# Attention matmuls in 64x64 tiles, and the fourth sequence loaded head by head, in a fused retention and feed-forward kernel

## The chip, the cores and the metric

The kernel runs on one core of a Trainium2 chip. The metric is the device time of one execution in microseconds (us), as the median of several runs. A core has five engines with instruction streams of their own: PE (TensorE, matrix products), DVE (VectorE), ACT (ScalarE), POOL (GpSimd) and SP (SyncE, which here only issues DMAs), and 16 DMA engines that they share.

## The reference

A decayed linear attention (retention) is followed by a feed-forward block with the activation h + sin(alpha h)^2 / alpha.

```python
# q, k, v: (4, 8, 768, 64) float32; gamma[h] = 1 - 2**(-5-h); scale = 1/8
for t in range(S):
    state = gamma * state + k[:, :, t] (outer) v[:, :, t]
    y[:, :, t] = scale * q[:, :, t] @ state
x = y as (4*768, 512)
h = x @ w_in                       # 512 x 2048
s = sin(alpha * h)
out = (h + s * s / (alpha + 1e-9)) @ w_out     # 2048 x 512
```

The recurrence is computed in chunks: within a chunk as masked scores times v, across chunks through a 64x64 state per head.

## The kernel before, in words

**Chunks and groups.** Each of the 4 sequences is cut into 6 chunks of 128 tokens, 24 chunks in all, for all 8 heads at a time. `order` (P in the code) holds the first chunk of each sequence (e0 to e3 = P[0] to P[3]), then the other five of sequence 0 (P[4] to P[8]), of sequence 1 (P[9] to P[13]), 2 and 3 (P[19] to P[23]). The feed-forward block works on seven groups of consecutive chunks of that order, of 4, 2, 4, 4, 4, 4 and 2 chunks. The order of instructions on each engine is written out by hand, with no scheduler.

**Attention of a chunk.** q and k are cast to bf16 on the way in and transposed to [2 heads x 64, 128 tokens], either on PE with an eviction (`half_T`, `stage_T`) or by a DMA transpose that SP issues (`turn`, X in the schedule). `stage_A` (L207, A) makes the scores, 8 matmuls that contract over 64 rows (L213), and DVE masks them out of PSUM into bf16 (L217). `stage_M` (L236, M) multiplies the state, held as a 128x128 block-diagonal matrix of two heads in bf16 (`s_bd`), with q (L247, 8 matmuls of 128 rows and 64 columns), adds the masked scores times v (L251, 8 matmuls), then adds k times v to the running state in a PSUM bank of its own (`stage_S`, L227, 8 matmuls). DVE scales the result by the decay table into xT (L258), and ACT copies the state to `s_bd` (L234, two copies of 64 partitions). v is multiplied beforehand by a decay factor (`scale_v`, L112), mostly on POOL. `SK` does the state sums of a sequence's first chunk.

**Feed-forward.** A `Slot` computes one tile of 128 hidden units for the tokens of a group: 4 matmuls into `ph` (L279), a sine on ACT (L282), a square on ACT or DVE (L287, L289), and one fused multiply-add on DVE into gT (L294, `add`), which frees `ph`. `ff_out` (L304) multiplies gT with w_out into a PSUM bank per chunk; `take` (L309) copies it out on ACT (L316) and SP stores it.

**Order.** `phase` (L375) runs the 16 slots of group g (for a group of 2 chunks, 8 double slots), spreads the output matmuls of group g-1 among them, and in given slots the attention of group g+1: A of a chunk and M of the one before it together, the last M in the last slot but one. Within a slot the order is: matmuls, sine, square, attention, add, output matmuls. Group 0 and what lies up to L515 is written out line by line.

**Loads.** POOL issues nearly all loads: 3 DMAs for a chunk (q, k, v; `load_chunk`), 4 for w_in (`load_w_in`), 4 for w_out. Every one of them reuses one of 8 semaphores and so waits for the landing of the load eight before it. After L486 the loads of P[7] and later chunks stand on POOL between the `scale_v` of earlier chunks.

**PSUM** has 8 banks: 4 rotating ones ("mm": ph, po, transposes), 2 for scores ("pa"), 1 for results and transposes ("ty") and 1 for the running state ("ps").

Of the kernel before, what the change touches and what calls it, by code (L numbers as in the profile page):

```python
# [11 lines left out]
ALU = mybir.AluOpType  # L12
# [3 lines left out]
def kernel(  # L16
# [9 lines left out]
):  # L26

# [45 lines left out]
    def load_chunk(j, names="qkv"):  # L73
        for name, src in (("q", q), ("k", k), ("v", v)):
            if name not in names:
                continue
            if name == "v":
                t = big.tile([128, H, D], BF16, name="vr", tag="vr", bufs=NJ)
            else:
                if ("qk", j) not in raw:  # L80
                    raw["qk", j] = big.tile([128, 2, H, D], BF16, name="qkr", tag="qkr", bufs=NJ)
                t = raw["qk", j][:, "qk".index(name)]
            nc.gpsimd.dma_start(out=t, in_=chunk_of(src, j))  # L83
            raw[name, j] = t

# [4 lines left out]
    def load_w_in(i):  # L90
        nc.gpsimd.dma_start(out=w_in[:, :, i * fw:(i + 1) * fw], in_=w_in_v[:, :, i * fw:(i + 1) * fw])
# [6 lines left out]
    for name, src in (("q", q), ("k", k)):  # L98
        near[name] = big.tile([128, H, D], F32, name=f"{name}0")
# [11 lines left out]
    def scale_v(j, eng):  # L111
        eng.tensor_mul(raw["v", j], raw["v", j], kg[:, j % NCH, :, None].to_broadcast([128, H, D]))  # L112
# [38 lines left out]
    for p in range(NP):  # L151
        for e in range(2):
            nc.vector.memset(lgp[64 * e:64 * e + 64, p:p + 1], lng[2 * p + e])
# [3 lines left out]
                         lg[:, None, :].to_broadcast([128, NCH, H]))  # L157
    qg = consts.tile([128, NCH, NP, C], F32, name="qg")
# [12 lines left out]
    s_bd = [big.tile([128, NP, 128], BF16, name=f"s_bd{i}") for i in range(2)]  # L171
# [3 lines left out]
    xT = {}  # L175

    def half_T(j, i, eng):
# [4 lines left out]
        for p in range(NP):  # L182
            nc.tensor.transpose(pt[:, p, :], raw["qk"[i], j][:, 2 * p:2 * p + 2, :].rearrange("p h d -> p (h d)"), ident)
# [6 lines left out]
    def stage_T(j, eng=None, tag="ty"):  # L190
        pt = psum.tile([128, 2 * NP, 128], BF16, name="pt", tag=tag, bufs=4 if tag == "mm" else 1)
        st["qkT", j] = work.tile([128, 2 * NP, 128], BF16, name="qkT", tag="qkT", bufs=6)
        for i in range(2):
            for p in range(NP):
                nc.tensor.transpose(pt[:, i * NP + p, :],  # L195
                                    raw["qk"[i], j][:, 2 * p:2 * p + 2, :].rearrange("p h d -> p (h d)"), ident)
# [5 lines left out]
    def turn(j):  # L202

        st["qkT", j] = work.tile([128, 2 * NP, 128], BF16, name="qkT", tag="qkT", bufs=6)
        nc.sync.dma_start_transpose(out=st["qkT", j], in_=raw["qk", j].rearrange("p i h d -> p (i h d)"))

    def stage_A(j):  # L207
        qkT = st["qkT", j]
        pa = psum.tile([128, 2, NP, 128], F32, name="pa", tag="pa")
        for p in range(NP):  # L210
            for e in range(2):
                r = slice(64 * e, 64 * e + 64)
                nc.tensor.matmul(pa[:, e, p, :], qkT[r, NP + p, :], qkT[r, p, :],  # L213
                                 start=(p == 0), stop=True, skip_group_check=True)
        aT = work.tile([128, 2, NP, 128], BF16, name="aT", tag="aT", bufs=2)
# [349 lines left out]
```

## Time and profile before

| What | Value |
|---|---|
| median of 8 runs | 219.27 us (218.33 to 219.78) |
| the profiled execution's own time | 218.33 us |
| its span, first to last instruction | 216.6 us |
| granted PE clock | 1.00 throughout |
| DMA | 24.67 MB; the core's DMA engines at 9 tenths or more in the first 21 of 40 slices |
| first feed-forward matmul | 15.3 us |
| first slot of group 1, group 2, group 3, group 4, group 5, group 6 | 47.2, 64.1, 90.0, 122.5, 154.7, 184.6 us |
| last PE matmul ends, about | 212.4 us |

In the profile, L12 is line 12 of the kernel before. Busy times are sums over the instructions of an engine; matmuls are pipelined, so that the time from one start to the next tells more than a duration. A line such as `101.03 0.29 PE L227 MATMUL ps<-vr,qkr 128*64 128x64 bf16 x8` is eight matmuls, the first of which starts at 101.03 us and the last of which ends 0.29 us later; 128*64 are the rows and columns of the array that they use, 128x64 the moving operand.

### The profile page before, as it was taken

The page shows a single profiled execution, that of the slowest core. Times are in us where ns is not written, and L with a number is a line of the kernel's source. Part 1 is how long each engine was busy: PE and PEld are TensorE (multiplying, and loading weights), DVE is VectorE, ACT ScalarE, POOL GpSimd, SP SyncE. Part 2 cuts the span into 40 slices and gives each one's busy share as a digit, 9 for nine tenths or more (in the row PEclk, how much of TensorE's full clock was granted, in tenths as well). Part 3 has the DMA queues.
Part 4 walks back from the last instruction along what each step waited for, and adds up shares of the span by engine and source line. Part 5 has one row for each costly group of instructions (what it writes and reads, how often), then busy time and mean ns, then how long its engine had stood idle before and what let it go on. Part 6 is the DMA issues. An engine that isn't in the chain of part 4 may idle for free.

```text
span 216.6 us, 4245 instructions
## 1 busy us (share of the span) xinstructions
PE 207.6 (96%) x1661; PEld 107.6 (50%) x1661; DVE 128.7 (59%) x213; ACT 162.6 (75%) x311; POOL 90.1 (42%) x105
## 2 busy tenths in 40 slices
PE   7899898999989999999999999999999999999992
PEld 3445543467754545445454545454544544556540
DVE  4688579859896777666367467367464655233300
ACT  7679786758988899788777867877868876766610
POOL 8975335899899895897871000000000000000000
PEclk9999999999999999999999999999999999999999
DMA  9999999999999999999997046125001101111121
GB/s 128 158 197 192 206 207 163 154 206 174 164 149 175 172 137 155 114 162 162 149 185 106 3 94 100 50 49 101 20 30 51 48 0 51 48 48 48 51 96 50
DMA packets 99508, 24.67 MB, mean 114 GB/s; under 512 B 92304, under 2 KB 96416, under 8 KB 99488
## 3 DMA queue, kind: packets, MB, share of 16 engines
q0 software_dynamic: 77024, 13.37, 83.6%
q1 hardware_dynamic: 22464, 11.02, 25.3%
q8 instruction: 13, 0.21, 0.5%
q14 instruction: 7, 0.06, 0.1%
HBM read 27.27 MB, written 6.29 MB: 155 GB/s over the span
## 4 chain that ended last, share of the span: by engine, by line
PE 74%; DMA 12%; POOL 4%; DVE 4%; ACT 2%; issue 1%; POOLq 0%
PE po L304 35%; PE ph L279 31%; DMA qkr<-in_k_dram 8%; DMA w_in<-in_moe_w_in_dram 4%; PE py L247 3%; PE pa L213 2%; POOL qkr L83 2%; PE py L251 2%; DVE aT L217 1%; POOL vr L83 1%; DVE xT L258 1%; PE ps L227 1%; DVE gT L294 1%; PE pt L195 1%; ACT s L282 1%
## 5 line engine op out<-in xcount | busy, mean ns | idle before, releaser
L294 DVE SCALAR_TENSOR_TENSOR gT<-s,rec_alpha,ph 128x512 bf16<-128x512 f32 (+3 forms) x120 | 74.2, 638 | 68.0 <-ACT s L287 67.4
L304 PE MATMUL po<-w_out,gT 128*128 128x512 bf16 x384 | 98.5, 380 | 0.6 <-DVE gT L294 0.6
L279 PE MATMUL ph<-xT,w_in 128*128 128x512 bf16 (+3 forms) x480 | 98.0, 337 | 0.6 <-DVE gT L294 0.2
L282 ACT ACTIVATE s<-ph,alpha_sb 128x512 f32<-128x512 f32 (+3 forms) x120 | 69.6, 601 | 32.9 <-PE ph L279 32.7
L279 PEld LDWEIGHTS <-w_in 128*128 128x128 bf16 x480 | 45.5, 98 | 42.1 <-issue 1.8
L287 ACT ACTIVATE s<-s 128x512 f32<-128x512 f32 (+1 forms) x94 | 58.4, 621 | 2.6
L304 PEld LDWEIGHTS <-gT 128*128 128x128 bf16 x384 | 35.2, 98 | 38.2 <-issue 0.6
L112 POOL TENSOR_TENSOR vr<-vr,kg 128x512 bf16<-128x512 bf16 x21 | 22.0, 1060 | 11.6 <-DMA vr<-in_v_dram 11.6
L217 DVE TENSOR_TENSOR aT<-pa,mask 128x1024 bf16<-128x1024 f32 x20 | 24.4, 1221 | 0.2 <-PE pa L213 0.2
L83 POOL DMA_DIRECT2D vr<-in_v_dram x24 | 21.8, 910 | 4.0 <-DMA w_in<-in_moe_w_in_dram 1.7
L83 POOL DMA_DIRECT2D qkr<-in_q_dram x23 | 21.3, 927 | 3.9 <-DMA w_out<-in_moe_w_out_dram 1.7
L83 POOL DMA_DIRECT2D qkr<-in_k_dram x23 | 20.6, 895 | 3.6 <-DMA w_out<-in_moe_w_out_dram 3.4
L234 ACT CAST s_bd<-ps 64x256 bf16<-64x256 f32 x40 | 14.3, 359 | 2.5 <-PE ps L227 2.2
L316 ACT COPY o_sb<-po 128x512 f32<-128x512 f32 x23 | 13.1, 576 | 4.0 <-PE po L304 3.9
L258 DVE TENSOR_TENSOR xT<-py,qg 128x512 bf16<-128x512 f32 x20 | 13.7, 684 | 2.2 <-PE py L251 2.1
L328 PE MATMUL spare<-warm 128*128 128x512 bf16 x28 | 9.8, 476 | 1.2 <-DVE warm L131 1.2
L213 PEld LDWEIGHTS <-qkT 64*128 64x128 bf16 x192 | 5.4, 94 | 9.3 <-issue 7.1
L251 PE MATMUL py<-aT,vr 128*64 128x128 bf16 x192 | 9.6, 220 | 0.4 <-DVE rec_alpha L366 0.2
L213 PE MATMUL pa<-qkT 64*128 64x128 bf16 x192 | 9.6, 219 | 0.4 <-ACT qkT L186 0.2
L247 PE MATMUL py<-qkT,s_bd 128*64 128x128 bf16 x160 | 8.3, 224 | 0.8 <-DVE xT L258 0.7
L247 PEld LDWEIGHTS <-s_bd 128*64 128x64 bf16 x160 | 5.5, 109 | 4.7 <-issue 2.0
L251 PEld LDWEIGHTS <-vr 128*64 128x64 bf16 x192 | 6.9, 110 | 1.3 <-issue 1.0
(59 smaller groups left out, 69.8 us busy)
## 6 DMA issues: line engine op xcount, KB each, us to landing
out_dram<-o_sb SPq DMA_DIRECT2D x24, 256.0 KB, 2.4
vr<-in_v_dram POOLq DMA_DIRECT2D x24, 128.0 KB, 5.9
qkr<-in_q_dram POOLq DMA_DIRECT2D x23, 128.0 KB, 5.6
qkr<-in_k_dram POOLq DMA_DIRECT2D x23, 128.0 KB, 5.8
w_in<-in_moe_w_in_dram POOLq DMA_DIRECT2D x4, 512.0 KB, 10.1
w_out<-in_moe_w_out_dram POOLq DMA_DIRECT2D x4, 512.0 KB, 14.5
q<-in_q_dram SPq DMA_DIRECT2D x1, 256.0 KB, 3.2
k<-in_k_dram SPq DMA_DIRECT2D x1, 256.0 KB, 4.6
```

The costliest lines, as they stand in the source:

```text
L83: nc.gpsimd.dma_start(out=t, in_=chunk_of(src, j))
L112: eng.tensor_mul(raw["v", j], raw["v", j], kg[:, j % NCH, :, None].to_broadcast([128, H, D]))
L213: nc.tensor.matmul(pa[:, e, p, :], qkT[r, NP + p, :], qkT[r, p, :], start=(p == 0), stop=True, skip_group_check=True)
L217: nc.vector.tensor_mul(aT.rearrange("p e n t -> p (e n) t"), pa.rearrange("p e n t -> p (e n) t"), m)
L247: nc.tensor.matmul(py[r, p, :], s_bd[c % 2][:, p, r], qkT[:, p, :], start=(p == 0), stop=True, skip_group_check=True)
L251: nc.tensor.matmul(py[64 * e:64 * e + 64, p, :], vs[:, 2 * p + e, :], aT[:, e, p, :], start=(c == 0 and p == 0), stop=True, skip_group_che ...
L258: nc.vector.tensor_mul(x, py, qg[:, c])
L279: nc.tensor.matmul(self.ph[:, m, :], w_in[:, i, f * 128:(f + 1) * 128], xT[g][:, i, self.lo:self.hi], start=(m == 0 and i == 0), stop=(i = ...
L282: nc.scalar.activation(out=self.s[:, m, :], in_=self.ph[:, m, :], func=ACTF.Sin, scale=alpha_sb[:, f:f + 1])
L287: nc.scalar.activation(out=self.s, in_=self.s, func=ACTF.Square)
L294: nc.vector.scalar_tensor_tensor(gT[self.g][:, f, self.lo:self.hi], self.s[:, m, :], rec_alpha[:, f:f + 1], self.ph[:, m, :], op0=ALU.mult ...
L304: nc.tensor.matmul(po[g, ts], gT[g][:, f, ts * C:(ts + 1) * C], w_out[:, f, :], start=(f == 0), stop=(f == FF - 1))
```

## The change

Heads get another place. Head 4b + 2m + e is worked on in PSUM bank b, and its 64 output columns lie in half b XOR e, so that the four products of one m (b = 0, 1 and e = 0, 1) use the four quadrants of the array. w_in's rows for heads 4 to 7 are loaded with their 64-partition halves swapped to match: three DMAs in place of one for each of the four parts of w_in. The state is kept in fp32 in SBUF (`s_f`, added to by DVE) and handed on in bf16 as plain 64x64 blocks (`s_n`).

For the five later chunks of the fourth sequence (`wide`), q, k and v are loaded head by head (24 DMAs of 64 partitions), with two sets of 64 tokens on the free axis. Their scores, products and sums are 64x64 tiles, the half of the scores above the diagonal is left out, and the state is a zero-padded 128x128 block (`s_w`), written by POOL.

Scores of a chunk, state product and products of the chunk before and the state sums form one `burst`. The evictions that follow it (`keep`: state sum, `mask`, `exit`: xT, `hand`: the bf16 state) are queued by `phase` in an order of its own for group 1 (`calm=False`): `hand` ahead of the next slot's sine, and the slot's addition ahead of mask and exit. The first state sums (`begin`) move into group 0. P[8] to P[10] are transposed on PE, and stage_T's evictions are on ACT but for e3 and P[6]. scale_v of most chunks goes to DVE, and POOL issues loads with fewer waits. The last output tile is made in three column pieces.

PSUM: 4 "mm", 2 "pa", 2 "py" (results and sums). Some lines without bearing on this are left out; "..." marks the place.

```diff
     def load_w_in(i):
-        nc.gpsimd.dma_start(out=w_in[:, :, i * fw:(i + 1) * fw], in_=w_in_v[:, :, i * fw:(i + 1) * fw])
+        c = slice(i * fw, (i + 1) * fw)
+        nc.gpsimd.dma_start(out=w_in[:, 0:2, c], in_=w_in_v[:, 0:2, c])
+        for y in range(2):
+            nc.gpsimd.dma_start(out=w_in[64 * y:64 * y + 64, 2:4, c], in_=w_in_v[64 - 64 * y:128 - 64 * y, 2:4, c])
+    def load_seq(bt):
...
+        for i, src in enumerate((q, k, v)):
+            for h in range(H):
+                r = slice(64 * (h // NP), 64 * (h // NP) + 64)
+                o = tv[r, :, h % NP, :] if i == 2 else tqk[r, :, i, h % NP, :]
+                nc.gpsimd.dma_start(out=o, in_=src[bt, h, C:, :].rearrange("(f i) d -> i f d", i=64))
...
+    def sums(j, py, base=256):
+        ks, vs = raw["k", j], raw["v", j]
+        for f in range(2 if wide(j) else 1):
+            for m in range(2):
+                for b, e in tiles4:
+                    o = py[half(e), b, base + 64 * m:base + 64 * m + 64]
+                    if not wide(j):
+                        h = 4 * b + 2 * m + e
+                        nc.tensor.matmul(o, ks[:, h, :], vs[:, h, :], ...
+                    else:
+                        nc.tensor.matmul(o, ks[half(b), f, 2 * m + e, :], vs[half(b), f, 2 * m + e, :], ...
+    def keep(j, py, base=256):
+        new = py[:, :, base:base + 128].rearrange("p b (m d) -> p m b d", m=2)
...
+            nc.vector.tensor_add(s_f, s_f, new)
+    def hand_on(j):
+        i = (j % NCH + 1) % 2
+        if not wide(j + 1):
+            nc.scalar.copy(s_n[i], s_f)
+            return
...
+        nc.gpsimd.tensor_copy(s[half(0), :, 0:4:3], s_f[half(0)])
+        nc.gpsimd.tensor_copy(s[half(1), :, 1:3], s_f[half(1)])
+    def inter(j):
...
+        for m in range(2):
+            if wide(j):
+                for b in range(2):
+                    nc.tensor.matmul(py[:, b, m * 128:(m + 1) * 128].rearrange("p (f i) -> p f i", f=2),
+                                     s[:, m, b, :], qkT[:, m:m + 5:4, half(b)], ...
+                continue
+            for b, e in tiles4:
+                nc.tensor.matmul(py[half(b ^ e), b, m * 128:(m + 1) * 128], s[half(e), m, b, :],
+                                 qkT[half(e), 2 * b + m, :], ...
+    def scores(j, tag="pa"):
...
+                for f in range(2):
+                    for e in range(2):
+                        nc.tensor.matmul(pa[half(f), e, p, :], qkT[half(e), NP + p, half(f)], qkT[half(e), p, :], ...
...
+    def burst(old, new, first=None):
+        inter(old)
+        return {**scores(new), **mix(old, first)}
...
+    def last_tile(g, ts):
+        lo = 0
+        for n in (d_model // 2, d_model // 4, d_model // 4):
...
     def phase(...):
         for n in range(FF // nf):
+            more, fresh = rest[0], {}
+            if not calm:
+                run(more, "hand")
             now = Slot(g, n * nf, nf=nf).sq("A")
+            run(more, "keep", "exit", "hand")
             for fn in att.get(n, ()):
-                fn()
-            now.add()
-            while done < no * (n + 1) * nf // FF:
+                fresh.update(fn() or {})
+            if calm:
+                run(fresh, "mask")
+                now.add()
+            else:
+                run(fresh, *(("keep", "exit") if n == FF // nf - 1 else ("keep",)))
+                now.add()
+                run(fresh, "mask", "exit")
...
+            while done < ((no - hold) * (n + 1) * nf // FF if n < FF // nf - 1 else no):
...
+    for j in (e0, e1, e2, e3):
+        scale_v(j, nc.vector)
     a = Slot(0, 0, (n3, n4), 4)
...
     a = Slot(0, 13)
+    begin(e0)
     b.sq("D").add()
...
     load_chunk(P[10])
     scale_v(P[8], nc.gpsimd)
-    scale_v(e1, nc.gpsimd)
...
+    load_chunk(P[11])
+    scale_v(P[9], nc.gpsimd)
+    load_chunk(P[12])
+    load_chunk(P[13])
+    for j in P[14:19]:
+        load_chunk(j)
+    load_seq(3)
...
+    stage_T(P[6])
     fill(3)
-    stage_A(P[5])
-    SK(e0)()
...
+    run(burst(P[4], P[5]), "keep", "hand", "mask", "exit")
+    fill(4)
+    stage_T(P[7], nc.scalar)
     fill(5)
-    stage_M(P[4])
-    fill(4)
-    stage_M(P[5])
+    more = burst(P[5], P[6])
+    run(more, "exit", "keep")
+    stage_T(P[8], nc.scalar)
+    run(more, "hand", "mask")
     fill(4)
     phase(1, outs,
-          {0: [T(P[6]), X(P[8])], 1: [A(P[6])], 2: [T(P[7]), X(P[9])], 3: [A(P[7]), M(P[6])], 4: [X(P[10])],
-           5: [A(P[8]), M(P[7])], 6: [X(P[11]), A(P[9]), M(P[8]), SK(e1)], 7: [M(P[9])]}, 2)
+          {1: [B(P[6], P[7])], 2: [T(P[9])], 3: [B(P[7], P[8])], 4: [T(P[10]), X(P[11])],
+           5: [B(P[8], P[9], e1)], 7: [B(P[9], P[10])]}, 2, calm=False, hold=6)
...
-    for fn in out_pieces(NG - 1, range(sizes[-1])):
+    for fn in out_pieces(NG - 1, range(sizes[-1] - 1)):
         fn()
+    last_tile(NG - 1, sizes[-1] - 1)
```

In the later groups a burst of chunks j and j+1 stands three slots ahead of each quarter's end, the DMA transpose of the chunk two further on two slots before it, and scale_v one slot before it (four in the fourth sequence, on POOL).

## The prediction

> **What bounds the kernel now.** I read the page's first and fourth parts, then TensorE's timeline matmul by matmul, then busy times by stage.
>
> ```profile
> PE 207.6 (96%) x1661; PEld 107.6 (50%) x1661; DVE 128.7 (59%) x213; ACT 162.6 (75%) x311; POOL 90.1 (42%) x105
> PE 74%; DMA 12%; POOL 4%; DVE 4%; ACT 2%; issue 1%; POOLq 0%
> ```
>
> TensorE is busy nearly always and carries 74% of the chain; DMA and POOL carry the head. A busy TensorE may still stream badly, so I take start-to-start times around one attention chunk of group 4 (columns: start, length, engine, line, tiles, shape, count):
>
> ```profile
> 99.28 1.03 PE L279 MATMUL ph<-xT,w_in 128*128 128x512 bf16 x4
> 100.23 0.40 PE L213 MATMUL pa<-qkT 64*128 64x128 bf16 x8
> 100.56 0.41 PE L247 MATMUL py<-qkT,s_bd 128*64 128x128 bf16 x8
> 100.81 0.39 PE L251 MATMUL py<-aT,vr 128*64 128x128 bf16 x8
> 101.03 0.29 PE L227 MATMUL ps<-vr,qkr 128*64 128x64 bf16 x8
> 101.26 1.04 PE L304 MATMUL po<-w_out,gT 128*128 128x512 bf16 x4
> ```
>
> The next feed-forward matmul starts at 102.13. A 512-column matmul costs 0.216 us (four from 101.26 in 0.87). So the chunk costs 102.13 - 99.28 - 8 x 0.216 = 1.12 us. Its parts: L251's eight matmuls take 0.22 us (100.81 to 101.03), while eight unpaired 128-column transposes (L195, in the chain at 48.27) take 0.45: half-array matmuls already run **two at a time**, 0.055 a pair. L227's eight of 64 columns: 0.29 long, 0.196 each, so (0.29 - 0.196) / 7 = 0.0134 us apart. Each change of tile shape costs about 0.1: 0.09 into L213 (100.14 to 100.23), 0.11 out of it (0.33 against 0.22), 0.12 out of L227 (0.23 against 0.11); first weights after one 0.03.
>
> The stages, cut where TensorE starts a slot (columns: stretch, length, busy PE, PEld, DVE, ACT, POOL, clock, DMA):
>
> ```profile
> 37.25:47.23 9.98, 9.84 (x113) 5.21 (x111) 8.31 (x10) 6.29 (x12) 9.04 (x11) 1.00 2.36 174
> 47.23:64.11 16.88, 16.26 (x226) 12.01 (x225) 14.06 (x25) 14.36 (x33) 15.47 (x17) 1.00 2.01 166
> 64.11:89.96 25.85, 25.43 (x216) 12.40 (x216) 18.50 (x25) 22.66 (x41) 21.66 (x24) 1.00 2.03 154
> 89.96:122.45 32.49, 32.49 (x266) 15.80 (x265) 18.67 (x24) 26.07 (x47) 20.54 (x22) 1.00 1.52 135
> 122.45:154.69 32.24, 32.24 (x257) 15.61 (x256) 18.70 (x24) 25.06 (x45) 0.00 (x0) 1.00 0.35 67
> 154.69:184.56 29.87, 29.87 (x186) 13.84 (x185) 15.38 (x20) 23.20 (x39) 0.00 (x0) 1.00 0.10 36
> ```
>
> Subtract the feed-forward matmuls (30, 16 + 64 half-width, 96, 128, 128, 128 of 0.216, half-width at 0.109): 3.5, 6.45, 5.1, 4.9, 4.6 and 2.25 us are left for attention, transposes and waits, 26.8 in all. That, and the tail, is what the change can touch. From 64 us on TensorE alone is the limit; before, loads matter too:
>
> ```profile
> 19.79 17.17 DMA qkr<-in_k_dram
> 37.00 0.40 PE pt L195 x4
> 59.44 0.68 DVE xT L258
> ```
>
> P[4]'s k lands at 36.96 and TensorE, waiting since 35.8, goes on at 37.0. Group 1's slots then lose about 0.9 us to DVE (L258 in the chain).
>
> **The change, part by part.** *Burst of an ordinary chunk.* The state product goes from 8 matmuls in pairs (0.22) to 8 in fours (0.11). The scores stay at 0.22: 16 matmuls in fours instead of 8 in pairs. L251's and L227's successors keep 0.22 and 0.11. Shape changes stay three (0.32), first weights come twice (0.06). Sum 1.04, 0.08 less than 1.12. Four at a time needs one start per 0.014 us, L227's measured pace; that all four quadrants overlap, no row shows. Bounds: 0 extra, or pairs only, 0.33 extra. I take 0, since pairs along rows (L213) and along columns (L251) both overlap here.
>
> The Trainium skill ("TensorEngine Tiling (Array Packing)", Gotcha 1: PSUM Pressure) says that different row tiles cannot access one PSUM bank at the same time. The new state product puts row halves e = 0 and 1 of one b into one bank, on different partitions, which no row here shows. By the rule it would go in pairs and cost 15 x 0.11 = 1.65 us more in all.
>
> *Burst of the fourth sequence.* State product at full array, four matmuls of 0.056 = 0.22, with no shape change ahead; scores and products 0.165 each (8 of 128 and 8 of 64 columns, in fours); sums 0.11; two shape changes 0.21; weights 0.03: 0.90. The 64-column ones would start 0.007 apart, which no row shows; at L227's 0.0134 the 32 of them add 0.22. Bounds 0.90 and 1.12; I take 1.0.
>
> The skill ("TensorE: Matmul & The Clock Gate", Part 1) gives a floor of about 25 ns start to start. L227's 13.4 contradicts it for column tiles, and the measurement decides. By the rule this burst would be some 0.5 us dearer.
>
> *Fewer pieces.* A group now has four closed bursts; before, five (scores alone, three full, L251 alone, 0.44 + 3 x 1.12 + 0.80) and extra sums. By stage:
> - 64.11 to 89.96: 4 x 1.04 = 4.15, and I keep 0.35 of wait (76.89, o_sb): 4.5, gain 0.65.
> - 89.96 to 122.45: 4.15 against 4.9, gain 0.75.
> - 122.45 to 154.69: 4 x 1.0 against 4.6, gain 0.6.
> - 154.69 to 184.56: 1.0 + 0.22 + 0.40 against 2.25, gain 0.6.
>
> *Transposes moved to TensorE.* P[8] to P[10] leave SP's DMA transposes: 3 x 0.45 = 1.35 on TensorE, 3 x 1.01 of copies on ACT. T(P[6]) moves ahead of the first burst and now waits for its load. Transfers follow P[4]'s k about 0.9 us apart (POOL's issues at 36.33, 37.24, 38.15, each released by a landing); P[6]'s k is six later: 37.0 + 5.4 = 42.4. TensorE would be there at 41.25 and wait about 0.95. Work from 37.25: scores alone 0.43, four transposes 1.8, two bursts 2.1, wait 0.95: 5.3 against 3.5, **loss 1.8**. Group 1's slots: 4 x 1.04 + 2 x 0.45, and 0.4 of waits I leave standing, 5.45 against 6.45: gain 1.0. The hold of six output matmuls gives DVE 1.7 us to finish L258's successor ahead of group 2; that removes the wait after 61.3.
>
> *Other engines.* Group 1's slots on ACT: 8 x 1.41 (two sines 0.87, square 0.54), two transpose copies 1.9, four hand-ons at 0.33 (one L234 cast's row), two o_sb 1.0: 15.4. TensorE needs 10.45 + 5.05 = 15.5: level. DVE: 16 x 0.39 + 4 x (1.14 + 0.60 + 0.35) = 14.6, the new 0.35 by the 256-wide rows. In group 2 DVE gains scale_v (0.61 clear of POOL's arithmetic, 1.44 beside it): 16 x 0.67 + 4 x 2.7 + 1.0 for the masks = 22.5 of 25.2. Level or hidden, but with no reserve. In the last groups scale_v and the state copies on POOL have at least four slots (7 us) before their use.
>
> *Head.* Eight more DMA issues on POOL (w_in in thirds, about 0.74 each, 5.9 us) all stand before P[4]'s. Cover: w_in and w_out land at DMA's pace, not POOL's; P[4]'s k was issued at 19.79 and landed 17 us later, so up to about 6 us are hidden. If a 64-partition transfer were half as fast, the eight halves would cost 5 us: no row; I take 0, as the packets are the same. begin(e0) (0.31) and a DVE state copy (0.35) lie in the wait before 37.0; four scale_v (2.4) fit DVE's idle 24.7 to 27.3. I put 0.2 for what leaks. The fourth sequence's 24 issues end near 95 us at 0.75 each; its first transpose comes near 112.
>
> *Tail.*
>
> ```profile
> 203.63 8.80 PE L304 MATMUL po<-w_out,gT 128*128 128x512 bf16 x40
> 212.46 0.42 DVE L313 COPY o_sb<-po 128x256 f32<-128x256 f32 x1 [6.23 <-PE po L304]
> 212.92 0.37 ACT L314 COPY o_sb<-po 128x256 f32<-128x256 f32 x1 [3.33 <-DVE o_sb L313]
> ```
>
> Two serial copies (0.83) become one of 128 columns (0.42 - 0.13 = 0.29); 48 narrower matmuls instead of 16 cost 0.1: gain 0.45.
>
> **Sum**: -0.65 - 0.75 - 0.6 - 0.6 - 1.0 - 0.45 + 1.8 + 0.2 = -2.05 us; with wide bursts between 0.90 and 1.0 and the 0.4 + 0.35 of kept waits as likely gone as not, -2.5. The profiled execution took 218.33 (span 216.6, 1.7 around it), so 215.8; the median of the eight runs is 0.94 higher, 219.27, so **216.8**.
>
> **Rivals.**
> - *Pairs only (slower).* If fours run two at a time: 15 ordinary bursts x 0.33 and about 1.6 in the wide ones, +6.5, net +4.0: 223.3. Against: rows and columns each overlap today. It decides once over 2.5 / 6.5 = 0.38 of the overlap is lost. Chance 0.10.
> - *Late weights (slower).* The split w_in lands P[4] 5 us later, 4.6 felt: 221.4. It decides from 2.9 us. For: all lies before 37 us. Against: same bytes. Chance 0.06.
> - *ACT or DVE takes over in groups 1 and 2.* Both are level with TensorE; 1.5 us more waits: 218.3. Chance 0.17.
> - *Better.* No wait at T(P[6]), 0.75 of waits gone, bursts of 0.90: 214.8. Chance 0.15.
> - Forecast, 215.9 to 218.2: chance 0.52.
>
> The range 214.6 to 220.0 leaves out half of "better" and nearly all of the two slower cases, 0.2. Faster by over 0.3% (what a measurement here can tell, 0.66 us): 0.52 + 0.15 + half of 0.17, 0.75; within 0.08; slower 0.17.
>
> **What would show it.** Starts in a burst: scores x16 in 0.22 and the state product in 0.11 after the change, else pairs. TensorE idle ahead of P[6]'s transposes near 42. Group 2's first slot near 64.5; groups 3 to 5 shorter by about 2 us together; the last copy 0.5 us sooner. Wrong if P[4]'s transposes start after 38, or if ACT or DVE is named ahead of TensorE's idle time after 65.

## The result and the profile after

The change makes the kernel slower: 222.76 us in the median of 11 runs (221.18 to 226.18) against 219.22 (218.33 to 222.12) for the kernel before, run on the same chip; the ratio is 1.013 (95% interval 1.011 to 1.016). The prediction was 216.8 us, with a range up to 220.0. The ratio leaves out the slow executions, those in which the granted clock dipped, and the profiled execution of the new kernel is one of them: 224.77 us (span 223.0), 2.0 above the median. Why it is that long is part of what follows: in it TensorE's clock dipped after a wait of the kernel's own.

Parts 1 and 4 of the new page, the lines that answer to the first two shown of before:

```profile
PE 208.4 (93%) x1929; PEld 110.2 (49%) x1929; DVE 143.1 (64%) x257; ACT 157.4 (71%) x290; POOL 90.1 (40%) x120
PE 68%; DMA 20%; POOL 4%; ACT 4%; DVE 3%; issue 1%; POOLq 0%; DVEq 0%
```

TensorE's share of the chain fell from 74% to 68% and DMA's rose from 12% to 20%; 5 of those points are the DMA transposes (`qkT<-qkr`), which do not appear in the chain of before. TensorE now waits for data in the middle of the kernel.

The matmuls themselves do what they were meant to. TensorE's timeline around one chunk of group 4 (L354 state product, L365 scores, L392 products, L313 sums):

```profile
109.08 1.03 PE L441 MATMUL ph<-xT,w_in 128*128 128x512 bf16 x4
110.03 0.31 PE L354 MATMUL py<-qkT,s_n 64*64 64x128 bf16 x8
110.17 0.39 PE L365 MATMUL pa<-qkT 64*64 64x128 bf16 x16
110.50 0.41 PE L392 MATMUL py<-aT,vr 128*64 128x128 bf16 x8
110.74 0.29 PE L313 MATMUL py<-vr,qkr 128*64 128x64 bf16 x8
110.97 0.39 PE L465 MATMUL po<-w_out,gT 128*128 128x512 bf16 x1
```

From start to start the eight of L354 take 0.14 us, the first weights with them, and the sixteen of L365 take 0.33, the change of shape with them: four run at a time. The burst costs 110.97 - 109.08 - 4 x 0.216 = 1.03 us, 1.12 before.

The same cut by stages as in the prediction, from the end of P[4]'s transposes to the first slots of groups 1 to 6 (stretch, length, busy PE, PEld, DVE, ACT, POOL, clock, DMA):

```profile
38.43:50.16 11.73, 11.13 (x159) 6.24 (x159) 9.15 (x14) 6.44 (x10) 10.67 (x13) 1.00 2.31 179
50.16:68.61 18.45, 15.84 (x258) 11.63 (x257) 14.79 (x28) 15.09 (x32) 17.59 (x20) 1.00 2.23 146
68.61:99.25 30.64, 27.03 (x257) 12.68 (x256) 23.56 (x38) 21.21 (x37) 18.59 (x25) 0.94 2.24 146
99.25:131.17 31.92, 31.92 (x289) 15.35 (x288) 23.14 (x33) 24.32 (x42) 6.83 (x10) 1.00 0.88 97
131.17:162.56 31.39, 31.39 (x325) 15.54 (x324) 19.84 (x29) 22.58 (x37) 6.28 (x11) 1.00 0.30 60
162.56:191.74 29.18, 29.18 (x201) 13.67 (x200) 14.35 (x20) 22.58 (x37) 1.83 (x3) 1.00 0.10 37
```

Beside the rows of before this gives the balance, in us:

| Stretch | before | after | difference | predicted |
|---|---|---|---|---|
| up to the end of P[4]'s transposes | 37.25 | 38.43 | +1.18 | +0.2 |
| from there to group 1 | 9.98 | 11.73 | +1.75 | +1.8 |
| group 1's slots | 16.88 | 18.45 | +1.57 | -1.0 |
| group 2's slots | 25.85 | 30.64 | +4.79 | -0.65 |
| groups 3 to 5 | 94.60 | 92.49 | -2.11 | -1.95 |
| the rest of the span | 32.0 | 31.2 | -0.8 | -0.45 |

The balance sums to 6.4 us, where the medians differ by 3.5: the profile of before is of its fastest execution (218.33 us), that of the new kernel of one above its median. Most of the first row, and the clock's part of group 2, belong to these two executions (before_split and the end of this section). Rows three and four hold the error: 2.6 and 5.4 us beyond what was predicted. Each has its wait, with a name:

```profile
PE pa L365 <- DMA qkT<-qkr: 2.4, 1, 2.4
PE py L354 <- DVE xT L405: 1.8, 2, 1.6
PE py L354 <- ACT qkT L258: 0.8, 1, 0.8
```

(PE's waits from 50 to 97 us, the three largest: who waits for what, us in total, times, longest. The other three, all in group 2, are 0.6 us for a `scale_v` on VectorE, 0.4 for the state and 0.2 for an output copy.) The longest wait for L405, in the timeline of group 1:

```profile
63.19 0.88 DVE L456 SCALAR_TENSOR_TENSOR gT<-s,rec_alpha,ph 128x256 bf16<-128x256 f32 x2 [0.69 <-ACT s L449]
63.27 1.03 PE L441 MATMUL ph<-xT,w_in 128*128 128x256 bf16 x8
63.97 1.22 DVE L369 TENSOR_TENSOR aT<-pa,mask 128x1024 bf16<-128x1024 f32 x1
65.11 0.68 DVE L405 TENSOR_TENSOR xT<-py,qg 128x512 bf16<-128x512 f32 x1
65.94 0.31 PE L354 MATMUL py<-qkT,s_n 64*64 64x128 bf16 x8 [1.63 <-DVE xT L405]
```

Read it from below. L354 opens the next burst and needs the one results buffer `py`, which L405 (the exit) frees. L405 stands behind the mask L369, that behind the addition L456, and L456 had itself waited 0.69 us for ScalarE's square. One after the other they outlast the slot. VectorE is busy only 14.79 of 18.45 us here: it is the order of its work that makes TensorE wait. TensorE has nothing else to do in this wait: of the output matmuls, the six that the diff holds back (`hold=6`) stand behind this burst. What the hold costs or gains no run shows.

The wait in group 2, from the timelines of SP's queue, then TensorE's:

```profile
69.42 0.34 SPq L473 DMA_DIRECT2D out_dram<-o_sb  x1
69.95 9.72 SPq L265 DMA_TRANSPOSE qkT<-qkr  x3
```

```profile
77.58 0.31 PE L354 MATMUL py<-qkT,s_n 64*64 64x128 bf16 x8
80.25 0.42 PE L365 MATMUL pa<-qkT 64*64 64x128 bf16 x16 [2.36 <-DMA qkT<-qkr]
81.70 1.06 PE L441 MATMUL ph<-xT,w_in 128*128 128x512 bf16 x2
```

P[12]'s k landed at 62.87. Its DMA transpose stands in SP's order behind the store of group 0's last output tile (69.42), goes out at 69.95, 7.1 us after that landing, and lands at 80.20, 10.2 us later. The scores of P[12] are due in slot 5 of group 2, at 77.7, 7.8 us after the issue. The same in before, SP's queue and then the scores of P[12], in slot 9:

```profile
65.15 0.33 SPq L317 DMA_DIRECT2D out_dram<-o_sb  x1
65.67 5.24 SPq L205 DMA_TRANSPOSE qkT<-qkr  x2
```

```profile
78.62 0.40 PE L213 MATMUL pa<-qkT 64*128 64x128 bf16 x8
```

There its k landed at 64.52; the transpose went out behind the same store, 1.2 us after that, landed at 72.09, 6.4 us later, and had 12.9 us until its scores.

After the idle stretch TensorE's clock falls: two matmuls of 512 columns from 81.70 take 0.43 us each instead of 0.216, the granted clock from 81.3 to 84.7 us is 0.50, and that of the whole stretch is 0.94.

### The profile page after: what moved, and what is told of

It reads as the page before. It is cut to its first block, busy times and chain, and to the rows that moved or that the text cites. A ratio compares the mean times of both kernels' runs of the same rounds, so it can differ in the third digit from the quotient of the medians.

```text
span 223.0 us, 4783 instructions
## 1 busy us (share of the span) xinstructions
PE 208.4 (93%) x1929; PEld 110.2 (49%) x1929; DVE 143.1 (64%) x257; ACT 157.4 (71%) x290; POOL 90.1 (40%) x120
## 4 chain that ended last, share of the span: by engine, by line
PE 68%; DMA 20%; POOL 4%; ACT 4%; DVE 3%; issue 1%; POOLq 0%; DVEq 0%
PE po L465 32%; PE ph L441 27%; DMA w_in<-in_moe_w_in_dram 7%; DMA w_out<-in_moe_w_out_dram 5%; DMA qkT<-qkr 5%; DMA qkr<-in_k_dram 3%; PE py L392 2%; POOL vr L89 2%; PE poh L483 2%; POOL qkr L89 2%; ACT s L444 1%; PE py L354 1%; PE pa L365 1%; ACT s L449 1%; DVE gT L456 1%
## 5 line engine op out<-in xcount | busy, mean ns | idle before, releaser
L456 DVE SCALAR_TENSOR_TENSOR gT<-s,rec_alpha,ph 128x512 bf16<-128x512 f32 (+3 forms) x120 | 74.4, 638 | 59.7 <-ACT s L449 59.5
L369 DVE TENSOR_TENSOR aT<-pa,mask 128x1024 bf16<-128x1024 f32 x15 | 18.3, 1221 | 2.4 <-PE pa L365 2.0
L89 POOL DMA_DIRECT2D vr<-in_v_dram x19 | 17.3, 909 | 2.8 <-DMA w_out<-in_moe_w_out_dram 1.2
L89 POOL DMA_DIRECT2D qkr<-in_q_dram x18 | 16.5, 916 | 1.7 <-DMA w_out<-in_moe_w_out_dram 1.2
L405 DVE TENSOR_TENSOR xT<-py,qg 128x512 bf16<-128x512 f32 x20 | 13.7, 684 | 1.3 <-PE py L313 1.3
L142 DVE TENSOR_TENSOR vr<-vr,kg 128x512 bf16<-128x512 bf16 x15 | 10.0, 685 | 0.0
L104 POOL DMA_DIRECT2D qk_seq<-in_q_dram x8 | 5.7, 714 | 8.7 <-DMA vr<-in_v_dram 5.7
L258 ACT COPY qkT<-pt 128x1024 bf16<-128x1024 bf16 x6 | 6.0, 1003 | 3.4 <-PE pt L256 3.4
L365 PE MATMUL pa<-qkT 64*64 64x128 bf16 x240 | 6.0, 217 | 2.4 <-DMA qkT<-qkr 2.4
L142 POOL TENSOR_TENSOR v_seq<-v_seq,kgq 128x512 bf16<-128x512 bf16 x5 | 5.2, 1040 | 6.5 <-DMA v_seq<-in_v_dram 6.2
L325 DVE TENSOR_TENSOR s_f<-s_f,py 128x256 f32<-128x256 f32 x16 | 6.7, 416 | 1.7 <-PE py L313 1.7
L354 PE MATMUL py<-qkT,s_n 64*64 64x128 bf16 x120 | 4.6, 227 | 3.0 <-DVE xT L405 1.8
```

The source lines that it names most:

```text
L142: eng.tensor_mul(t, t, by[:, j % NCH, :, None].to_broadcast([128, H, D]))
L365: nc.tensor.matmul(pa[half(f), e, p, :], qkT[half(e), NP + p, half(f)], qkT[half(e), p, :], start=(p == 0), stop=True, skip_group_check=True)
L369: return {"mask": lambda: nc.vector.tensor_mul(aT.rearrange("p e n t -> p (e n) t"), pa.rearrange("p e n t -> p (e n) t"), mask_bc)}
L405: more = {"exit": lambda: nc.vector.tensor_mul(x_of(j), py[:, :, 0:256].rearrange("p b (m t) -> p b m t", m=2), qg[:, c].rearrange("p (b m ...
L456: nc.vector.scalar_tensor_tensor(gT[self.g][:, f, self.lo:self.hi], self.s[:, m, :], rec_alpha[:, f:f + 1], self.ph[:, m, :], op0=ALU.mult ...
```

## The experiments

Each is the new kernel with an edit, unless it says otherwise, and was timed against the kernel before on the same chip. "Group 1" and "group 2" are the lengths of these stretches in the profile (before: 16.87 and 25.86 us).

### again: the new kernel once more

> The changed kernel once more, unaltered, for a profile without a lowered clock. Theory: the loss lies ahead of 100 us, in three pieces: P[4]'s load a good 1 us later (the split w_in), waits of 2 to 3 us in group 1's slots (the one results buffer is freed late, because mask and xT product queue behind the addition), and a wait of 1 to 3 us for the DMA transpose of P[12] in group 2's slots. The three should be there again: ahead of the scores of P[12] over 1 us, and group 1's slots over 18 us. Rival: the wait for P[12] belongs to the one disturbed execution and is under 0.5 us here; then another 2 us must be found.

223.49 us, ratio 1.017 (1.011 to 1.022); group 1 18.45, group 2 30.32, a wait of 2.3 us for the same DMA transpose, the clock 0.94 in group 2 again. The wait is not an accident of one execution.

### exit_first: the exit ahead of the addition in group 1

```diff
-                run(fresh, *(("keep", "exit") if n == FF // nf - 1 else ("keep",)))
+                run(fresh, "keep", "exit")
                 now.add()
-                run(fresh, "mask", "exit")
+                run(fresh, "mask")
```

> The changed kernel with one alteration: in group 1's double slots the xT product goes ahead of the slot's addition in every slot, the mask stays behind it. Theory (the results buffer waits for the xT product, which waits for a square it does not need): the state product no longer waits in group 1, its slots fall from 18.4 to about 16.5 us, and the time falls by 1.5 to 2 us. Rival (ACT is full in group 1 with the transposes' evictions, and DVE's order only shows it): the slots stay within 0.5 us and the waits move to the feed-forward matmuls.

222.25 us, ratio 1.011 (1.008 to 1.014). Group 1 falls from 18.45 to 17.17, group 2 stays at 30.55. VectorE's work is the same and only its order differs, so 1.3 of the 1.57 us that group 1 lost are the order. The whole time shows less of it: the ratio's interval overlaps that of the new kernel (1.011 to 1.016). What is left is a wait of 0.9 us, now for the mask (L369), which frees the one scores buffer.

### pe_turn: P[12] and P[13] transposed by TensorE

```diff
-                at(a - 2, X(P[n + 2]))
+                at(a - 2, T(P[n + 2]) if n + 2 < 14 else X(P[n + 2]))
```

> The changed kernel with P[12] and P[13] transposed on TensorE (eviction on ACT) instead of by SP's DMA, in the same slots. Theory (their loads are there in time, at 67.6 and 70.4 us for k, but the DMA transpose takes 10 us behind POOL's loads): the wait of 2.5 us ahead of P[12]'s scores goes, at 0.9 us of TensorE and 2 us of ACT; net -1 to -2.5 us, more where the wait also lowered the clock. Rival (the loads themselves are late): the wait moves to the transposes and the time stays within 0.5 us.

221.26 us, ratio 1.007 (1.005 to 1.009). Group 2 falls from 30.3 to 27.25, though TensorE has two transposes of 0.45 us more to do; no wait for a DMA transpose is left there and the clock stays at 1.00. (The landings of k that the expectation names, 67.6 and 70.4, are those of P[13] and P[14] in the new kernel; P[12]'s landed at 62.87.)

### throttle: scale_v back on POOL between the loads

```diff
-    load_chunk(P[12])
-    load_chunk(P[13])
-    for j in P[14:19]:
-        load_chunk(j)
+    for n in range(12, 19):
+        load_chunk(P[n])
+        scale_v(P[n - 2], nc.gpsimd)
...
-            at(a - (4 if wide(j) else 1), V(j))
+            if n > 16:
+                at(a - (4 if wide(j) else 1), V(j))
```

> The changed kernel with scale_v of P[10] to P[16] back on POOL between the loads, as before the change (each waits for its v to land and holds back the loads behind it), and off DVE. Theory (POOL's loads, issued without these pauses, crowd the DMA transposes): the transposes of P[12] and P[13] land in 6 to 7 us instead of 10 to 11, the wait in group 2's slots falls below 1 us, the time falls by 1 to 2 us. Rival (the transposes are slow for what they are, or the deadline came nearer since scores now run a burst ahead): latencies stay at 9 us or more and nothing is won; POOL's later loads then may cost up to 1 us more.

220.44 us, ratio 1.004 (1.002 to 1.006); group 2 25.96. The transposes keep their place and number, but the one of P[12] now takes 6.6 us and lands at 77.1, a microsecond ahead of the scores (SP's queue, then TensorE's timeline):

```profile
70.54 6.92 SPq L265 DMA_TRANSPOSE qkT<-qkr  x3
```

```profile
78.17 0.31 PE L354 MATMUL py<-qkT,s_n 64*64 64x128 bf16 x8
78.31 0.39 PE L365 MATMUL pa<-qkT 64*64 64x128 bf16 x16
```

The scores follow 0.14 us behind the state product. So the latency of this transpose comes with POOL's loads: without `scale_v` between them POOL issues them one behind the other. In the new kernel loads issued from 70.9 to 75.3 landed 11.7 to 14.3 us later (6.1 to 7.7 for those issued from 59 to 68), where those for k issued from 59.4 to 68.2 in before landed after 5.1 to 5.9. In whole, mask_first and three, which keep this edit, P[12]'s transpose took 7.3 to 8.4 us, in again and exit_first 10.2 and 10.4. The expectation held for P[12] alone: the next two transposes still took 10.6 and 9.2 us, but nothing waited for them. The edit also takes seven `scale_v` off VectorE, and with them TensorE's wait for one of these (0.3 us in again). It brings group 2 from 30.3 (again) to 25.96, 0.1 over before; some 1.5 us of this is the clock, which stays at 1.00 here.

### before_split: the kernel before, w_in loaded in three DMAs per part

```diff
-        nc.gpsimd.dma_start(out=w_in[:, :, i * fw:(i + 1) * fw], in_=w_in_v[:, :, i * fw:(i + 1) * fw])
+        c = slice(i * fw, (i + 1) * fw)
+        nc.gpsimd.dma_start(out=w_in[:, 0:2, c], in_=w_in_v[:, 0:2, c])
+        for y in range(2):
+            nc.gpsimd.dma_start(out=w_in[64 * y:64 * y + 64, 2:4, c], in_=w_in_v[64 * y:64 + 64 * y, 2:4, c])
```

> The kernel before, with each of its four w_in loads cut in three as in the change (two row blocks over 128 partitions, then two halves of 64 partitions, each to its own place). Theory (the cut alone delays the first weights, since the first six pieces reach the DMA engines late; the later pieces lose nothing): P[4]'s k lands 1 to 2 us after the 36.95 of the kernel before, and the time rises by 0.8 to 1.8 us. Rival (the delay comes from something else in the head, the new tables or the tiles that q and k of chunk 0 now share with the output): P[4]'s k lands within 0.4 us of 36.95 and the time stays.

219.36 us, ratio 0.999 (0.997 to 1.001). The split costs nothing that can be measured, and the theory that it delays the head falls. Here P[4]'s k lands at 37.82; in the twelve profiles of the new kernel and its variants that record it, it lands between 37.59 and 38.94, in tail (below), whose head is that of before, at 38.30, and in the profiled execution of before at 36.95. That execution was before's fastest (218.33); the 1.2 us at the head of the balance above are mostly this spread between executions.

### whole: throttle, with w_in loaded in one DMA per part

```diff
-        nc.gpsimd.dma_start(out=w_in[:, 0:2, c], in_=w_in_v[:, 0:2, c])
-        for y in range(2):
-            nc.gpsimd.dma_start(out=w_in[64 * y:64 * y + 64, 2:4, c], in_=w_in_v[64 - 64 * y:128 - 64 * y, 2:4, c])
+        nc.gpsimd.dma_start(out=w_in[:, :, c], in_=w_in_v[:, :, c])
```

> The run with scale_v back on POOL, and w_in loaded in four DMAs of 128 partitions again; the swap of partition halves is left out, so heads 4 to 7 meet the wrong rows of w_in (same work, other numbers). Theory: the counterpart of the kernel before with the cut; P[4]'s transposes start at 36.1 to 36.9 instead of 38.4 and the ratio to the kernel before falls from 1.004 by 0.005 to 0.008. Rival (64-partition pieces or their number cost nothing): P[4] stays at 38 and the ratio at 1.004.

This leaves out the swap of the halves. 220.25 us, ratio 1.002 (1.000 to 1.005), against 1.004 (1.002 to 1.006) for throttle; the intervals overlap widely. Same answer as before_split from the other side.

### mask_first: throttle, with the mask ahead of the addition in group 1

```diff
                 run(fresh, *(("keep", "exit") if n == FF // nf - 1 else ("keep",)))
+                run(fresh, "mask")
                 now.add()
-                run(fresh, "mask", "exit")
+                run(fresh, "exit")
```

> The run with scale_v back on POOL, and in group 1 the mask ahead of the slot's addition, the xT product still behind it (the change's own order is addition, mask, xT product). Theory (what matters is when the xT product frees the results buffer; it is behind mask and addition in both orders): group 1's slots stay within 0.6 us of 18.45. Rival (the addition ahead of the mask is itself the loss): they fall by over 1.5 us, as far as with the xT product first (17.2).

220.44 us, ratio 1.004 (1.002 to 1.007); group 1 17.93, 0.5 under throttle, group 2 26.64, 0.7 over it. Nothing is won in all. The exit's place matters more than the mask's (exit_first: 1.3).

### three: throttle, exit_first and two more moves

```diff
                 now.add()
-                run(fresh, "mask", "exit")
+                run(fresh, *(("mask", "hand") if n == FF // nf - 1 else ("mask",)))
...
-    stage_T(P[6])
-    fill(3)
+    fill(7)
     run(burst(P[4], P[5]), "keep", "hand", "mask", "exit")
-    fill(4)
+    stage_T(P[6])
     stage_T(P[7], nc.scalar)
```

> The run with scale_v back on POOL, with three more alterations: in group 1 the xT product ahead of the addition (group 1's slots 18.4 to 17.2 alone), the last hand-on of group 1 in its own slot (0.5 us wait in group 2's second slot), and P[6]'s transposes behind the first burst (up to 0.6 us of wait for its load). Theory, the sum: 1.3 + 0.5 + 0.4 = 2.2 us off 220.4, which is 218.3, just under the kernel before. Rival (ACT is full in group 1, so that waits only change places): under 1.2 us is won, 219.2 or more.

219.59 us, ratio 1.000 (0.998 to 1.003): level with before. Group 1 17.17, group 2 26.60. With the two waits repaired, the late gains of 2.9 us only pay for the longer stretch ahead of group 1 (11.76 us from the slot behind P[4]'s transposes, 9.91 in before_split), the late load and what is left in groups 1 and 2.

### turns: three, with P[8] to P[10] by DMA transposes as in before

```diff
     more = burst(P[5], P[6])
-    run(more, "exit", "keep")
-    stage_T(P[8], nc.scalar)
-    run(more, "hand", "mask")
+    run(more, "exit", "keep", "hand", "mask")
+    X(P[8])()
...
-          {1: [B(P[6], P[7])], 2: [T(P[9])], 3: [B(P[7], P[8])], 4: [T(P[10]), X(P[11])],
+          {0: [X(P[9])], 1: [B(P[6], P[7])], 2: [X(P[10])], 3: [B(P[7], P[8])], 4: [X(P[11])],
```

> The run three (219.59 us, level with before), and P[8], P[9] and P[10] turned by SP's DMA transposes again, as before the change, in place of TensorE's. Theory (these three moved transposes are a real loss of the change, as the prediction had it, and their copies on ScalarE feed the 0.86 us wait in group 1): TensorE saves 3 x 0.45 = 1.35 us and some 0.4 us of that wait, so about 217.9 us, 0.8% under before; the stretch from P[4]'s transposes to group 1 shortens by 0.45 and group 1 from 17.17 to about 15.9 us. Rival (a DMA transpose beside POOL's loads takes 6 to 10 us from issue to landing): P[9]'s k lands near 53.0 in three, so its transpose lands between 59 and 63, and the scores that need it come at about 61.5; TensorE then waits up to 1.2 us for each and the time stays near 219.3.

219.73 us, ratio 1.001 (0.999 to 1.003), not the 217.9 of the theory. The transpose that left the stretch ahead of group 1 gave its 0.44 us (from the start of P[4]'s transposes 12.35 instead of 12.79). The two of 0.45 that left group 1 gave 0.39 together (16.78), and group 2 took 0.3 more, with a wait of 0.9 us for P[11]'s DMA transpose. The timeline of group 1 shows what has come in their place:

```profile
55.83 1.22 DVE L369 TENSOR_TENSOR aT<-pa,mask 128x1024 bf16<-128x1024 f32 x1
57.10 0.42 PE L365 MATMUL pa<-qkT 64*64 64x128 bf16 x16 [0.81 <-DVE aT L369]
```

TensorE waits 1.6 us in three places for the mask. So the theory fails for group 1: there the moved transposes lay mostly beside VectorE's chain. The time came out near the rival's, but not by its reason: these transposes were not late; P[11]'s was.

### turns_more: transposes issued two slots sooner, begin(e0) later

```diff
-          4: [X(P[11])],
+          4: [X(P[11])], 6: [X(P[12])],
...
-            if n + 2 < NJ:
-                at(a - 2, X(P[n + 2]))
+            if 12 < n + 2 < NJ:
+                at(a - 4, X(P[n + 2]))
...
-    begin(e0)
     b.sq("D").add()
     F((0, 1), (9,))
     b = Slot(0, 14)
-    hand_on(e0)
     a.sq("A").add()
     F((0, 1), (10,))
+    begin(e0)
     stage_T(P[4], nc.scalar)
     a = Slot(0, 15)
+    hand_on(e0)
```

> As turns, and two more moves: the DMA transposes of P[12] and later chunks issued two slots sooner (P[12]'s in slot 6 of group 1), and the first state sum of group 0 (begin) behind the output matmuls ahead of P[4]'s transposes, where DVE's state copy doesn't delay an addition. Theory (what is left of the loss in group 2 is the transposes' lead, not their number): the 0.91 us wait at 76.5 goes, and up to 0.4 us ahead of P[4]'s transposes; about 1.0 us under turns, so 216.9. Rival (the transposes' latency grows with the loads that they are issued among, so a sooner issue lands no sooner): within 0.3 us of turns.

220.02 us, ratio 1.001 (0.999 to 1.004), within 0.3 us of turns as the rival had it. The later `begin` did shorten the way to group 1 by 0.5 us (from the start of P[4]'s transposes 11.82 instead of 12.35), but TensorE now waits 1.0 us ahead of these transposes for VectorE's addition. The sooner transpose of P[12], ahead of the store in SP's order and issued at 66.1, landed at 75.4, in time. But the wait of 0.9 us in turns, at 70.96, was for P[11]'s, not for P[12]'s as the theory had it; issued at 62.1 and landed at 71.3, it grew to 1.7.

### tail: the kernel before, with the last output tile in three pieces

```diff
-    for fn in out_pieces(NG - 1, range(sizes[-1])):
+    for fn in out_pieces(NG - 1, range(sizes[-1] - 1)):
         fn()
+    last_tile(NG - 1, sizes[-1] - 1)
```

> The kernel before, and of the change only the last output tile computed in three column pieces. Theory (the late part of the prediction held: from TensorE's last matmul to the end of the span 4.1 us before and 3.3 after, with 0.1 us of narrower matmuls): 0.5 to 0.75 us under before, a ratio near 0.997. Rival (the gain belongs to the other late edits, and 48 narrower matmuls and two more stores eat it): level with before.

218.53 us against 219.55, ratio 0.995 (0.993 to 0.997). Of all parts of the change this one, alone, is worth 1.0 us. The last two lines on VectorE in its timeline:

```profile
213.00 0.29 DVE L333 COPY o_sb<-poh 128x128 f32<-128x128 f32 x1 [5.47 <-PE poh L327]
213.89 0.29 DVE L333 COPY o_sb<-poh 128x128 f32<-128x128 f32 x1 [0.60 <-PE poh L327]
```

Two pieces are copied and stored while TensorE still works on the next, and a copy of 0.29 us ends the kernel where two serial ones took 0.83.

### best: turns_more, with P[11] transposed by TensorE

```diff
-          4: [X(P[11])], 6: [X(P[12])],
+          6: [T(P[11]), X(P[12])],
```

> As turns_more, with P[11] turned by TensorE in slot 6 of group 1 instead of by a DMA transpose. In turns_more that transpose was issued at 62.1, when P[11]'s k had landed, and landed at 71.3; TensorE waited 1.6 us for it at 69.3. Theory (the wait belongs to this one transpose's latency of 9 us): TensorE pays 0.45 us, beside waits for VectorE, and saves the 1.6: group 2 falls from 27.3 to about 25.8, time about 218.6. Rival (P[12]'s transpose, landed at 75.2, is late next, since the scores that need it then come at about 74.5): group 2 stays above 26.5 and the time near 219.5.

218.70 us, ratio 0.996 (0.994 to 0.999), under both kernels. The two middle stretches (columns as above):

```profile
50.07:67.23 17.16, 15.76 (x249) 11.31 (x248) 15.04 (x29) 14.40 (x31) 17.16 (x20) 1.00 2.05 163
67.23:92.68 25.45, 25.02 (x257) 12.25 (x256) 20.73 (x34) 20.87 (x36) 19.34 (x22) 1.00 2.08 146
```

Group 2 is at 25.45, 0.4 under before and 0.25 over the 25.2 that the prediction had for it. TensorE is busy 25.02 of it. Group 1 is still above before.

### best_all and no_mask: what else holds group 1

best_all is best with all of VectorE's work for a burst ahead of the addition:

```diff
-                run(fresh, "keep", "exit")
+                run(fresh, *(("keep", "exit", "mask", "hand") if n == FF // nf - 1 else ("keep", "exit", "mask")))
                 now.add()
-                run(fresh, *(("mask", "hand") if n == FF // nf - 1 else ("mask",)))
```

> As best, and in group 1 VectorE runs a burst's state addition, exit and mask all ahead of the slot's addition, which waits for ScalarE's square. Theory (in group 1 the buffers of scores and results come free too late because they stand behind that addition): the waits at the bursts, 1.6 us in turns, fall under 0.6, group 1 from 16.8 to about 15.8, time about 217.6. Rival (VectorE's work is the limit, and its order only moves the wait to the feed-forward part, as with the mask ahead of the addition before): group 1 stays within 0.4 us of 16.8.

219.23 us, ratio 1.001 (0.998 to 1.003); group 1 18.42 instead of 17.16. The wait for the mask is gone, but 1.2 us of wait for the addition (L456) and 1.6 us for P[9]'s DMA transpose have come; that transpose was issued at 52.3 and landed at 61.5, in best at 52.6 and 59.2.

no_mask is turns with the scores of P[7] to P[10] copied by ScalarE, the mask left out:

```diff
+            if j in P[7:11]:
+                return {"mask": lambda: nc.scalar.copy(aT, pa)}
```

> As turns, but in group 1's four bursts the scores are copied out by ScalarE without the mask (this part of the computation is left out), so VectorE has 4 x 0.6 us less to do there. In turns group 1 took 16.78 us although three transposes had left TensorE, and TensorE waited 1.6 us in it for VectorE's mask instruction to free the single scores buffer. Theory (group 1 is held by VectorE: 15.05 of 16.78 us busy, its chain of state addition, exit, addition, mask one behind the other): group 1 falls to about 15.2 us and the time to about 218.2. Rival (the loads hold group 1, and the wait for the mask only shows their lateness): ScalarE takes 4 x 0.6 us more and group 1 stays within 0.4 us of 16.8.

220.47 us, ratio 1.005 (1.001 to 1.008); group 1 18.81 instead of 16.78. TensorE waits no longer for VectorE, but 3.3 us for the transposes of P[9] (landed at 61.4) and P[10] (66.2), 1.4 and 2.7 us later than in turns. This does not tell VectorE's chain from the loads: the landing of the transposes moved with it. What holds group 1 above 16.8 once the exit is out of the way stays open; the runs show two things at the same level there, VectorE's chain and the DMA transposes under the loads, and that relieving one brings out the other.

## Why the prediction was wrong, step by step

- **The bursts: right.** 1.04 us predicted for an ordinary one, 1.03 measured. The rival "pairs only" is out: sixteen score matmuls take 0.33 us, shape change included. The 64-column matmuls of the fourth sequence start 7 ns apart on average (four in 0.029 us), and its burst takes 0.92 us of start-to-start time where 1.0 was taken and 0.90 was the lower bound.
- **The two rules of the Trainium skill that were weighed: the trace disagrees with both.** The state product puts two row halves into one bank and runs four at a time, eight matmuls in 0.14 us with the first weights ("TensorEngine Tiling (Array Packing)", Gotcha 1). And 7 ns stand against the floor of about 25 ns from start to start ("TensorE: Matmul & The Clock Gate", Part 1); on one quadrant the starts lie 29 ns apart or more, so it is between quadrants that the floor does not hold.
- **Groups 3 to 5: right.** -1.95 predicted, -2.11 measured (-0.57, -0.85, -0.69).
- **The tail: right, undersized.** -0.45 predicted, -0.8 in the balance, and 1.0 us when measured alone.
- **The stretch ahead of group 1: right.** +1.8 predicted, +1.75 measured, with another make-up: busy TensorE grew by 1.29 us (9.84 to 11.13, near the three transposes' 1.35) and idle time by 0.46, where 0.85 and 0.95 were predicted: that the sum agrees is luck, since the two errors cancel. The wait for a load of k is 0.5 us in the trace.
- **The head: right, but for the execution.** In the balance +1.18 stands against +0.2. P[4]'s transposes end 0.3 us after the landing of its k in before and 0.48 after it in the new kernel; the other microsecond is the landing itself, which differs between executions (38.30 in tail). The 0.94 us that the prediction added to get from its execution to the median covers this. The rival "late weights" is out (before_split). In three and turns TensorE waits another 0.4 us behind these transposes for VectorE's addition, which stands behind `begin`'s state copy.
- **Group 1: the step failed.** The prediction said "5.45 against 6.45: gain 1.0", with 0.4 us of waits left standing, and called VectorE "level or hidden". Its total was right (14.6 predicted, 14.79 measured). What it left out is the diff's own order: keep, addition, mask, exit, with one results buffer that the exit frees and an addition that first waits for ScalarE. The waits came to 2.6 us; exit_first gets 1.3 us of the stretch back by order alone. The other 1.3 us, between the 17.17 of exit_first and the 15.9 that the prediction had, stay open. The rival "ACT or DVE takes over" named the place, and priced it at 1.5 us; the prediction's own sign of being wrong, VectorE named ahead of TensorE's idle time after 65, came at 65.94.
- **Group 2: the step failed, and it is the larger one.** The prediction said "4 x 1.04 = 4.15, and I keep 0.35 of wait (76.89, o_sb): 4.5, gain 0.65". It counted TensorE's work and VectorE's, and never asked when the inputs of the scores land. Three things meet here: the scores are due four slots sooner, `scale_v` leaves POOL so that its loads run unspaced, and the transpose stands in SP's order behind a store that came 6.6 us after the landing of its k, 0.6 us in before. From issue to use it had 7.8 us, where before had 12.9, and it took 10.2 instead of 6.4: by these numbers neither the sooner use nor the longer latency alone makes it late.

  The prediction counted the second only as work that VectorE gains (and at 0.61 us each, which no row of a `scale_v` has; undisturbed it takes 0.68). Spacing the loads again (throttle) takes back 4.4 us of what again lost in this stretch, two transposes on TensorE (pe_turn) 3.1; in the medians, from 222.76, it is 2.3 and 1.5. What the store costs no run shows by itself; issued at 62.87, when k was there, and with the same 10.2 us, the transpose would have landed near 73.1, in time, which is an estimate. Of the 4.8 us some 1.5 are the clock after the wait (the ten matmuls of 512 columns from 81.70 to 85.35 took 3.65 us where ten of 0.216 take 2.16).

Both cases in which the prediction had a slower kernel, "pairs only" and "late weights", are out; it is slower by a third that the prediction did not have, the lateness of the inputs. Without the two failed waits the sum comes nearer: in best, group 2 stands at the prediction and the late groups beat it, and it runs 0.8 us ahead of before (0.996 of 219.25), where 2.5 were forecast. The rest is group 1 and the stretch ahead of it. The tail alone gives as much (0.995, with overlapping intervals): no run here shows a net gain from the rearrangement ahead of it.

## What to carry to other kernels

Ask of each step that is moved sooner when its inputs land, not only how long it takes: list the lead of each transfer (issue, place in its queue, landing, first use) before and after the change. Here POOL's arithmetic between its DMA issues spaced the loads, and taking it away lengthened loads and transposes alike; so look at what stands between the issues before moving it. Look also at what an issue stands behind in its queue: P[12]'s transpose stood 7.1 us behind a store while its data were there. And where one buffer is freed by the last of several instructions on an engine, add them up as a chain from the matmul that fills it to the one that needs it; that the engine is idle a fifth of the time, as VectorE was here, says nothing about it.

## What the runs showed of the hardware

- Matmuls on the four 64x64 quadrants overlap fully: four of 128 columns every 0.056 us, the time that one such transpose on the full array takes (eight in 0.45), and four of 64 columns in 0.029 us.
- A DMA transpose of one chunk took 5.8 to 7.4 us from issue to landing in before (those issued from 56 to 69 us), and 10.2 to 11.4 us in the new kernel (those issued from 70 to 75 us), beside unspaced loads, of which those issued from 71 to 75 us took 12 to 14 us. From 132 us on, with the loads over, it took 3.1 to 4.8 us in the new kernel.
- In the three profiles with a TensorE wait of 2.3 to 2.5 us in group 2 (the new kernel, again, exit_first) the granted clock of that stage was 0.94, and 512-column matmuls took 0.43 us for a while; in the new kernel the clock was 0.50 for 3.4 us. In the other profiles it was 1.00 there, in turns_more after a wait of 1.7 us and in no_mask, in group 1, after one of 1.9 too. A long wait cost more than its length.
- Loading w_in in twelve DMAs, eight of them of 64 partitions, instead of four cost nothing measurable (ratio 0.999).
